# Three real products per complex spectrum product, a head start for the first 256 tokens, and convolution steps handed out by VectorE time

## The chip, the cores and the metric

One core of a Trainium2 chip. The time is device microseconds of one execution, as the median of a few. A profile is one more execution, traced; its span is close to the timed one, not equal. Several chips were used, and the kernel before took 746 to 751 us (medians) on them, so kernels of different sessions are compared by their ratio to the kernel before of the same rounds.

In the profile lines PE is TensorE, PEld its loading of weights, DVE is VectorE, ACT ScalarE and POOL GpSimd; L306 is line 306 of the kernel. In a row of digits each digit is the busy share, in tenths, of one of 40 equal slices of the span. The granted clock (PEclk) is the share of TensorE's full clock that the profile recorded; a cold clock is one of about 0.50. An eviction copies a result out of the memory in which TensorE accumulates.

## The reference

A gated long convolution and then a gated MLP, for 2048 tokens of width 576, hidden width 4608. Cut to what matters:

```python
def _A_ref(q, k, v, shift_k, ssm_k, ssm_D):          # convolution part
    k_shift = sum_t k_pad[:, t:t+S] * shift_k[:, 3-t]
    kv = k_shift * v
    y = irfft(rfft(kv, 2S) * rfft(ssm_k, 2S))[:S] + kv * ssm_D
    return q * y
mod = (silu(c) @ w_mod)                               # six rows: sa, ca, ga, sb, cb, gb
h = layernorm(x) * (1 + ca) + sa
x = x + ga * _A_ref(h, k, v, ...)
h = layernorm(x) * (1 + cb) + sb
x = x + gb * ((silu(h @ w1) * (h @ w3)) @ w2)         # MLP part
```

## The kernel before

The tokens are cut into 8 blocks of 256. The causal convolution is done block by block: TensorE transforms each block of kv to a spectrum X and each block of the long kernel to V, VectorE multiplies X[j] by V[s-j] for each j and sums into the accumulators of block s, and TensorE transforms back. Old spectra are kept in DRAM and read again. The MLP runs in 4 rounds of 512 tokens: 36 hidden blocks (10 matmuls of 512 columns for gate and up together, then silu on ScalarE and the product on VectorE) and a down stage of 288 matmuls of 288 columns. Beside round r's MLP the convolution of round r+1 is threaded in: it is a generator, and the MLP takes a fixed number of its steps after each block.

```python
# one complex product by four real ones: 2304-wide and 1152-wide operations
nc.vector.tensor_mul(p1[:], X[:], V[:])
if not first: nc.vector.tensor_add(a[:], a[:], p1[:])
yield
nc.vector.tensor_mul(p2[:, 0:4:2, :], X[:, 0:4:2, :], V[:, 1:4:2, :])
nc.vector.tensor_mul(p2[:, 1:4:2, :], X[:, 1:4:2, :], V[:, 0:4:2, :])
if not first: nc.vector.tensor_add(b[:], b[:], p2[:])
yield
# ... cut ...
for fc in range(NF // FC):
    for fi in range(FC):
        # ... 10 matmuls, silu, copy, product ...
        interleave(self.rate)            # 2 steps after each hidden block
for h in range(2):
    for f0 in range(0, NF, W2C):         # W2C = 6, two buffers of down weights
        # ... 24 matmuls ...
        interleave(self.rate2)           # 1 step after each down chunk
```

In round 2 there are 72 steps, so two for each of 36 blocks use up all of them beside the hidden stage. A step is anything from an eviction to 2.6 us of VectorE work.

## Time and profile before

| | before |
|---|---|
| median (lowest to highest) | 746.39 us (745.03 to 750.81), 4 runs |
| profiled span | 753.8 us |
| TensorE busy, mean granted clock | 567.0 us, 0.889 |
| VectorE busy | 388.8 us |
| prologue, then the four rounds | 86, 166, 185, 194, 123 us |

A round's length is read from the first gate matmul of one round to that of the next (86.5, 252.0, 437.1 and 630.9 us). The last round has no convolution beside it and so shows what the MLP alone needs.

### The profile page before, as it was taken

Reading aid. Unit: us, or ns where it says so; the run is one execution under the profiler, and the core shown is the slowest. Engines: PE = TensorE matmul, PEld = TensorE weight load, DVE = VectorE, ACT = ScalarE, POOL = GpSimd, SP = SyncE. Lnnn points to the kernel's source line nnn. Section 1 sums busy time; section 2 is a strip of 40 time slices with the busy share of each in tenths; the row PEclk is TensorE's granted clock in tenths of the full one; section 3 lists DMA queues with packets and bytes.
Section 4 is the critical chain, followed back from the end, with each engine's and each line's share of the span. In section 5 each row is a group of like instructions: output and inputs, shape, how many; then the busy total and the mean of one; then the engine's idle time right before and its main releaser. Section 6 shows DMA issues by size and latency. Waiting matters only on the chain.

```text
span 753.8 us, 8712 instructions
## 1 busy us (share of the span) xinstructions
PE 567.0 (75%) x3163; PEld 319.7 (42%) x3201; DVE 388.8 (52%) x708; ACT 254.0 (34%) x503; POOL 24.8 (3%) x44
## 2 busy tenths in 40 slices
PE   0385499549899979815969898984077889999996
PEld 0253244224367534302427654431033565444574
DVE  5668554799301264799940134299998112221111
ACT  3334455333510345314440054522144102445300
POOL 3001000000000000000100000000010000000000
PEclk9867699868999989966889999995579799999999
DMA  8873068713345649841325454694123246544153
GB/s 248 260 245 101 5 193 276 234 31 95 94 134 135 193 148 280 278 135 31 95 63 134 134 173 119 204 266 142 56 60 97 64 126 172 143 128 142 40 140 103
DMA packets 144255, 107.78 MB, mean 143 GB/s; under 512 B 6994, under 2 KB 134868, under 8 KB 144212
## 3 DMA queue, kind: packets, MB, share of 16 engines
q1 hardware_dynamic: 144064, 106.63, 48.2%
q10 hardware_dynamic: 148, 0.59, 0.2%
q8 instruction: 25, 0.41, 0.2%
q14 instruction: 18, 0.15, 0.1%
HBM read 97.17 MB, written 10.03 MB: 142 GB/s over the span
## 4 chain that ended last, share of the span: by engine, by line
PE 41%; DVE 35%; DMA 15%; issue 3%; ACT 3%; POOL 2%; POOLq 0%; SPq 0%; DVEq 0%; ACTq 0%
PE ps L477 24%; PE ps L496 11%; DMA w2t<-in_B_w_dram 10%; DVE zb L313 5%; DVE za L308 4%; PE ps L230 4%; DVE p L306 4%; DVE h L483 2%; DVE p L311 2%; DVE p L310 2%; DMA V<-Vd 2%; POOL l2r L351 2%; DVE xn L366 1%; DVE xn L364 1%; DVE kvt L249 1%
## 5 line engine op out<-in xcount | busy, mean ns | idle before, releaser
L477 PE MATMUL ps<-h2T,wst 128*128 128x512 bf16 x1402 | 340.9, 398 | 12.4 <-ACT u L482 6.2
L477 PEld LDWEIGHTS <-wst 128*128 128x128 bf16 x1440 | 146.5, 102 | 186.6 <-issue 36.8
L480 ACT ACTIVATE sg<-ps 128x512 bf16<-128x512 f32 x144 | 85.9, 596 | 364.6 <-PE ps L477 277.0
L496 PE MATMUL ps<-w2t,h 128*128 128x288 bf16 x1152 | 149.4, 289 | 15.0 <-DMA w2t<-in_B_w_dram 14.8
L483 DVE TENSOR_TENSOR h<-sg,u 128x512 bf16<-128x512 bf16 x144 | 60.8, 423 | 156.4 <-ACT u L482 156.4
L496 PEld LDWEIGHTS <-h 128*128 128x128 bf16 x1152 | 113.5, 99 | 50.3 <-issue 14.5
L504 DVE TENSOR_TENSOR og<-ps,gbrow 128x288 bf16<-128x288 f32 x32 | 13.2, 452 | 143.4 <-PE ps L496 143.4
L482 ACT CAST u<-ps 128x512 bf16<-128x512 f32 x144 | 83.7, 581 | 0.0
L384 PE MATMUL ps<-za,Fb 128*128 128x288 bf16 x64 | 15.7, 333 | 58.4 <-DVE za L374 58.4
L398 PE MATMUL ps<-ident,h2row 128*128 128x128 bf16 x80 | 10.4, 287 | 48.2 <-DVE h2row L367 48.2
L230 PE MATMUL ps<-kv,Fb 128*128 128x288 bf16 x128 | 21.8, 325 | 30.2 <-ACT Fb L139 18.7
L384 PEld LDWEIGHTS <-Fb 128*128 128x128 bf16 x128 | 13.7, 111 | 67.9 <-DVE za L374 61.0
L306 DVE TENSOR_TENSOR p<-X,V 128x2304 bf16<-128x2304 bf16 x28 | 37.9, 1352 | 0.1
L313 DVE TENSOR_TENSOR zb<-zb,p 128x2304 bf16<-128x2304 bf16 x28 | 37.8, 1352 | 0.0
L308 DVE TENSOR_TENSOR za<-za,p 128x2304 bf16<-128x2304 bf16 x28 | 37.8, 1351 | 0.0
L230 PE MATMUL ps<-kT,Fk 128*128 128x288 bf16 x128 | 22.0, 317 | 16.4 <-DVE kT L272 14.8
L341 ACT ACTIVATE junk<-x 128x576 bf16<-128x576 bf16 x32 | 21.9, 685 | 25.1 <-DVE x L390 18.5
L398 PEld LDWEIGHTS <-h2row 128*128 128x128 bf16 x80 | 6.8, 127 | 55.6 <-DVE h2row L367 54.9
L230 PEld LDWEIGHTS <-Fb 128*128 128x128 bf16 x128 | 13.8, 109 | 37.9 <-ACT Fb L139 18.6
L233 ACT CAST W<-ps 128x576 bf16<-128x576 f32 x32 | 19.8, 654 | 20.2 <-PE ps L230 20.1
L351 POOL TENSOR_TENSOR l2r<-l2v,neghalf 128x1 f32<-128x1 f32 x16 | 12.6, 790 | 371.4 <-DVE l2v L350 371.4
L233 ACT CAST X<-ps 128x576 bf16<-128x576 f32 x32 | 19.3, 656 | 13.9 <-PE ps L230 13.9
(81 smaller groups left out, 356.5 us busy)
## 6 DMA issues: line engine op xcount, KB each, us to landing
wst<-in_B_w_dram SPq DMA_DIRECT2D x144, 256.0 KB, 3.4
w2t<-in_B_w_dram SPq DMA_DIRECT2D x48, 432.0 KB, 3.5
X<-Xd SPq DMA_DIRECT2D x15, 576.0 KB, 3.7
V<-Vd SPq DMA_DIRECT2D x12, 576.0 KB, 5.6
kh<-in_A_k_dram SPq DMA_DIRECT2D x7, 720.0 KB, 5.4
wst<-in_B_w_dram SPq DMA_DIRECT2D x144, 32.0 KB, 3.0
Vd<-V SPq DMA_DIRECT2D x7, 576.0 KB, 6.2
h<-in_w_mod_dram SPq DMA_DIRECT2D x6, 576.0 KB, 7.9
```

Source lines behind the costliest of these rows:

```text
L230: nc.tensor.matmul(ps[:, h, 0:H], basis[:, cc, cs, e, :], rhs[:, cc, h * H:(h + 1) * H], start=(cc == 0), stop=(cc == 1))
L233: nc.scalar.copy(dst[:, 2 * e + cs, :].rearrange("p (h d) -> p h d", h=2), ps[:, :, 0:H])
L306: nc.vector.tensor_mul(p1[:], X[:], V[:])
L308: nc.vector.tensor_add(a[:], a[:], p1[:])
L313: nc.vector.tensor_add(b[:], b[:], p2[:])
L351: nc.gpsimd.tensor_tensor(rstd[:], var[:], self.neghalf[:, 0:n], op=ALU.pow)
L384: nc.tensor.matmul(ps[:, h, 0:H], self.Fb[:, e, cs, cc, :], z[:, 2 * e, h * H:(h + 1) * H], start=(e == 0 and cs == 0), stop=(e == 1 and c ...
L477: nc.tensor.matmul(gu[:, i, :], w[:, 5 * i + ct, fi * P:(fi + 1) * P], hT[:, ct, :], start=(ct == 0), stop=(ct == 4))
L480: nc.scalar.activation(sg[:], gu[:, 0, :], ACT.Silu)
L482: nc.scalar.copy(u[:], gu[:, 1, :])
L483: nc.vector.tensor_mul(self.h3[:, f, :], sg[:], u[:])
L496: nc.tensor.matmul(accs[t // 2][:, t % 2, 0:H], self.h3[:, f0 + f, t * P:(t + 1) * P], w[:, f, :], start=(f0 + f == 0), stop=(f0 + f == NF ...
```

## The change

Four things are meant to help: fewer VectorE operations for each complex product (three real products need one sum more for X and two for V, and their spectra have 6 rows instead of 4); steps that carry their VectorE cost, handed out in proportion to the MLP's time; the second block of 256 tokens moved from the prologue to beside the first 20 hidden blocks, which run on the first 256 tokens alone (their weights are read a second time for the other 256); and four smaller buffers for the down weights. The new order of the convolution also puts products that need no new X first. The K transpose's copy moves to ScalarE and the small statistics to GpSimd.

```diff
-W2C = 6
+W2C = 4
+NW2 = 4
+N1 = 20
     def pair(self, X, V, s):
-        nc.vector.tensor_mul(p1[:], X[:], V[:])
-        ... (five operations and two steps, as above)
+        p = self.prod.tile([P, 6, D], BF16, name="p", tag="p")
+        nc.vector.tensor_mul(p[:], X[:], V[:])
+        yield 2.0
+        nc.vector.tensor_add(z[:], z[:], p[:])
+        yield 2.0
     def kv_block(self, s):
+        nc.vector.tensor_add(X[:, 0:6:3, :], X[:, 1:6:3, :], X[:, 2:6:3, :])
     def k_block(self, s):
-        nc.vector.tensor_copy(kT[:], pt[:, :, 0:D])
+        nc.scalar.copy(kT[:], pt[:, :, 0:D])
+        nc.vector.tensor_add(V[:, 2:6:3, :], V[:, 0:6:3, :], VS)
+        nc.vector.tensor_sub(V[:, 1:6:3, :], VS, V[:, 0:6:3, :])
+    def advance(self, cost):
+        self.due += cost
+        while self.due > 0 and self.steps is not None:
+            c = next(self.steps, None)
+            ...
+            self.due -= c
     # after each hidden block, and after each down chunk:
-                interleave(self.rate)
+            self.advance(rate * (t1 - t0) / RB * 2.16)
-                interleave(self.rate2)
+                self.advance(rate * W2C * 4 * 0.126)
     def run(self):
-        for _ in self.conv(0):
+        for _ in self.conv_first():
             pass
+        self.begin(self.conv_second())
+        for fc in range(n1):
+            self.hidden(0, fc, 0, 256, 27.0 / (N1 * 1.08 * 0.9))
+        self.end()
         for r in range(NRB):
-            self.mlp(r, self.steps(r + 1))
+                cost = 4 * (2 * s0 + 1) + 42
+            time = 114.0 * 0.93 - (N1 * 1.08 if r == 0 else 0)
+            rate = cost / time
             ... (cut: hidden blocks, the second half of the first 20, down)
```

## The prediction

> **What bounds the kernel now.** I read the page's busy shares and its slices first, then the engines' busy time by stretch, then the groups of instructions, then the chain of waits in order of time.
>
> ```profile
> PE 567.0 (75%) x3163; PEld 319.7 (42%) x3201; DVE 388.8 (52%) x708; ACT 254.0 (34%) x503; POOL 24.8 (3%) x44
> ...
> PE   0385499549899979815969898984077889999996
> ...
> DVE  5668554799301264799940134299998112221111
> ...
> PEclk9867699868999989966889999995579799999999
> ```
>
> No engine is full over the span, but the two rows of digits are each other's mirror: where VectorE shows 9, TensorE shows 4 to 6 and its clock falls; where TensorE shows 9, VectorE shows 0 to 2. The work alternates, although the code means it to overlap. The stretches (start:end, length, then busy time of PE, PEld, DVE, ACT, POOL, the granted clock, the DMA share, GB/s) put numbers on it. The first five are the prologue and the four rounds of 512 tokens; two convolution-heavy stretches and the hidden stage of the last round follow.
>
> ```profile
> 0.00:87.00 87.00, 34.54 (x202) 23.13 (x204) 61.75 (x129) 33.89 (x67) 11.38 (x27) 0.78 0.61 185
> 87.00:250.00 163.00, 134.59 (x758) 75.47 (x767) 80.84 (x147) 58.62 (x116) 4.22 (x5) 0.91 0.49 142
> 250.00:437.00 187.00, 141.72 (x792) 79.18 (x801) 106.00 (x185) 61.42 (x124) 4.61 (x6) 0.89 0.51 149
> 437.00:631.00 194.00, 142.32 (x778) 78.85 (x786) 118.66 (x193) 61.43 (x124) 4.61 (x6) 0.85 0.45 132
> 631.00:754.00 123.00, 113.81 (x641) 63.08 (x646) 21.57 (x56) 38.65 (x72) 0.00 (x0) 1.00 0.43 122
> 308.00:342.00 34.00, 13.03 (x58) 5.46 (x58) 33.86 (x39) 7.44 (x14) 0.00 (x0) 0.79 0.57 173
> 488.00:543.00 55.00, 26.62 (x105) 10.90 (x105) 54.30 (x62) 12.20 (x23) 0.00 (x0) 0.72 0.57 169
> 631.00:706.00 75.00, 74.63 (x343) 33.97 (x348) 15.69 (x38) 36.50 (x68) 0.00 (x0) 1.00 0.47 133
> ```
>
> The last round, with no convolution beside it, takes 123 us. The three before take 163, 187 and 194. In 488 to 543 VectorE is busy for 54.3 of 55 us and TensorE gets 26.6 us done at a clock of 0.72. VectorE has only 119 us of work in that round of 194: it is the bound for a part of each round and idle in the rest.
>
> ```profile
> L306 DVE TENSOR_TENSOR p<-X,V 128x2304 bf16<-128x2304 bf16 x28 | 37.9, 1352 | 0.1
> L313 DVE TENSOR_TENSOR zb<-zb,p 128x2304 bf16<-128x2304 bf16 x28 | 37.8, 1352 | 0.0
> L308 DVE TENSOR_TENSOR za<-za,p 128x2304 bf16<-128x2304 bf16 x28 | 37.8, 1351 | 0.0
> ...
> L311 DVE TENSOR_TENSOR p<-X,V 128x1152 bf16<-128x1152 bf16 x28 | 21.0, 752 | 0.0
> L310 DVE TENSOR_TENSOR p<-X,V 128x1152 bf16<-128x1152 bf16 x28 | 21.0, 751 | 0.0
> ```
>
> These five are one accumulated spectrum product. The chain of waits steps through them at 1.27 and 0.67 us (each starts 0.08 us before the last ends), and at the down stage it alternates between matmuls and weight loads:
>
> ```profile
> 708.74 2.95 PE ps L496 x24
> 711.71 3.42 DMA w2t<-in_B_w_dram
> 715.17 3.11 PE ps L496 x24
> 718.30 3.54 DMA w2t<-in_B_w_dram
> ```
>
> Two buffers of six row blocks are used up in 6.2 us, while a freed one is refilled only 3.4 us later: a small hole in every second chunk.
>
> **What the Trainium skill says.** "VectorE: DVE Perf Modes", section "The perf-mode tier table", gives tensor_tensor on bf16 in SBUF two elements a cycle and one with a PSUM operand. The trace agrees: (1352 - 752) / 1152 = 0.52 ns an element, and 0.15 us fixed; the 576-wide product that reads PSUM takes 754 ns against 452. So 3456 elements cost about 0.15 + 3456 x 0.52 = 1.95 us, 1.87 as a step of the chain. "TensorE: Matmul & The Clock Gate", section "The HAM clock gate", says that an idle window of about 3.4 us halves the clock; the trace has 0.72 in the VectorE-bound stretch and 1.00 in the last round. "GPSIMD Engine Reference", section "Elementwise — side-by-side cycle accounting", names two software dispatch hops for each GpSimd instruction; the trace has 0.70 to 0.79 us for a power of one or two elements, against 0.15 us for a small VectorE operation. "DMA: Bandwidth & Descriptors", section "Issuing engines are not separate DMA queues", says that all transfers share 16 engines; here 0.47 of them move 133 GB/s of gate and up weights, so about 283 GB/s is all that this kind of load can get.
>
> **The change part by part.**
>
> *Products.* An accumulated product goes from 3 x 1.27 + 2 x 0.67 = 5.15 us to 2 x 1.87 = 3.74. There are 28 of them: 39 us less. The 8 first products go from 2.61 to 1.87: 6 us less. Against this stand a sum for each X (8 x 0.67) and two more operations for each V (16 x 0.67): 16 us more. The K transpose's copy goes to ScalarE (5 us off VectorE) and the small statistics to GpSimd (96 operations of 0.15, 15 us off). VectorE should go from 389 to about 340 us. If VectorE bound everything, this alone would be worth 49 us; the larger effect is the spreading.
>
> *Rounds.* With VectorE off the path, a round is TensorE's: hidden 77.4 us (the last round's, 631.3 to 708.7 in the chain), down 288 x 0.130 = 37.4 (3.12 us for 24 in the chain), and the convolution's own matmuls, two blocks of 48 x 0.1225 + 20 transposes x 0.108 = 16.1 in all (the chain steps through 8 transforms in 0.98 us and 10 transposes in 1.08). Sum 131 us, 115 for the last. VectorE's work beside it is at most about 110 us in round 2 and less before, so it fits if it is spread. The new order of VectorE's instructions does so: one 1.87 us step after each gated product of 0.34 us, 2.2 us per block against TensorE's 2.16. That is nearly balanced, with no clump.
>
> *First 256 tokens alone.* The prologue had both blocks, to 87 us. Now it is block 0 alone, after the modulation matmuls, which wait for 2 MB of weights (transfers issued by 12 us, 7.9 us to land, so about 20 us). I add: transpose and copy of K 5 us, two forward transforms with evictions 8, V and X sums and the product 5, inverse 3, gate, statistics, norm and transpose 10: about 51 us. Then 20 blocks at 256 columns: 200 matmuls of 0.108 = 21.6 us, and 8 us of convolution matmuls. VectorE has 26 operations of 0.67, four of 1.87, 20 small products of 0.21 and some 4 us of others there, about 33 us, and the chain at the end (statistics on ScalarE, five GpSimd operations, norm, transposes) is not covered: I take 40 us. So the second block is ready near 91 us, as late as before, but with 21.6 us of MLP done.
>
> *Second half of those 20 blocks.* Weights are loaded once more, 5.9 MB. A pair of blocks needs 0.59 MB per 2.2 us, 268 GB/s of my 283, and the convolution's own loads come on top: 6 us of waiting.
>
> *Down weights.* Four buffers of four blocks: the 3.4 us of a load lie beside 6.2 us of work. The hole goes: about 3 us a round.
>
> Sum in profile time: 91 for the start; round 0: 34.5 + 22 + 37.4 + 16.1 + 6 + 8 = 124; round 1: 131 + 8 + 2 = 141; round 2: 131 + 8 + 6 = 145; last 117. Total 618. The 8 is a round boundary: the last norm's chain is about 10 us with only 4 us of matmuls left to cover it, and the next x waits for the output to leave (in the old chain 3.15 + 4.20 us). The 2 and 6 are for spectra, which grow by half to 864 KB; in round 2 ten of them come in some 46 us, 193 GB/s on top of the weights' 0.47. The timed runs are 0.991 of the profiled span, so 612; I chose 606, because part of the boundary waits should overlap.
>
> **Rivals.** (1) DMA becomes the bound: the rows above already have 0.57 in product stretches; with spectra half as large again and the step 27% shorter, the demand nearly doubles. Against it: the average over the new span is only some 122 MB / 610 us = 200 GB/s. If it binds in rounds 1 and 2 throughout, 640 to 660. (2) VectorE stays the bound, since sg and u have two buffers and ScalarE waits for VectorE: a delay of one step stops the MLP. The 2.2 against 2.16 speaks for it, the room in the down stages against it: 625. (3) The small operations on GpSimd and the in-order queues lengthen each block's tail: five at 0.5 to 0.8 us, and matmuls placed behind a late transpose stand still: 10 us more at the boundaries. (4) All waits hide: 91 + 110 + 131 + 131 + 115 = 578, timed 573.
>
> **Range and chances.** Predicted 606 us, 8 times in 10 within 580 to 640. Low is nearly rival 4, high is rival 1 half true. Even all rivals together stay far below 746.9, since a round would have to lose over 35 us to them: faster by over 2% 0.98, within 2% 0.01, slower 0.01.
>
> **What would show it.** VectorE's busy time near 340 us, the product and sum rows near 1.95 us, 28 each. Round lengths near 124, 141, 145, 117, with no stretch of VectorE at 9 beside TensorE at 4. First 256-column matmul near 51 us, first 512-column one near 91. Mean clock nearer 0.95 than 0.89. Waits on down weights gone. I am wrong if the rounds stay above 155 us, if the longest waits of TensorE are for spectra or weights, or if the first 512-column matmul comes after 100 us.

## The result, and the profile after

| | before | after |
|---|---|---|
| median (lowest to highest), 4 runs each | 746.39 us (745.03 to 750.81) | 621.99 us (618.59 to 631.15, the last one slow) |
| ratio | 1 | 0.831, 95% interval 0.8255 to 0.8364 |
| profiled span | 753.8 us | 620.6 us |
| VectorE busy | 388.8 us | 341.9 us |
| mean granted clock | 0.889 | 0.956 |

A ratio is the mean time of one kernel's runs over that of the other's of the same rounds, so not quite the ratio of the medians. Executions over 1.5% slower than the fastest of the same kernel are left out of the means. First the page of the changed kernel, busy shares and slices:

```profile
PE 544.3 (88%) x3401; PEld 334.6 (54%) x3401; DVE 341.9 (55%) x534; ACT 268.6 (43%) x551; POOL 45.3 (7%) x104
...
PE   1738858898989698999998788999997979999997
...
DVE  5776576548493457819884338993976131121111
...
PEclk9957989999998989999998979999998989999999
```

The mirror is gone: from the seventh slice on TensorE shows 6 or more in every slice, also where VectorE shows 8 or 9. The same stretches as before, cut at the first matmuls of the changed kernel's stages (prologue, first 256 tokens, rest of round 0, rounds 1 to 3, then 60 us with products in round 2):

```profile
0.00:50.00 50.00, 22.30 (x134) 14.87 (x135) 32.59 (x62) 20.92 (x40) 14.21 (x36) 0.83 0.86 248
50.00:100.50 50.50, 38.47 (x305) 30.30 (x304) 30.67 (x56) 29.86 (x76) 4.90 (x13) 0.89 0.78 237
100.50:216.00 115.50, 104.62 (x751) 72.55 (x749) 70.28 (x114) 49.78 (x113) 6.12 (x15) 0.98 0.80 239
216.00:358.50 142.50, 132.28 (x785) 76.64 (x785) 89.84 (x126) 64.71 (x126) 10.14 (x20) 0.97 0.69 214
358.50:501.50 143.00, 132.13 (x784) 76.70 (x784) 98.33 (x125) 64.70 (x126) 9.89 (x20) 0.97 0.61 184
501.50:620.60 119.10, 114.51 (x648) 63.49 (x647) 20.15 (x52) 38.64 (x72) 0.00 (x0) 0.99 0.42 118
366.00:426.00 60.00, 58.37 (x290) 27.74 (x288) 50.15 (x54) 33.69 (x64) 3.63 (x5) 1.00 0.79 246
```

Rounds 1 and 2 took 185 and 194 us and take 142.5 and 143. In the product stretch VectorE is busy for 50.2 of 60 us, and TensorE for 58.4 at full clock: both at once, where before it was one or the other. The product rows, two where there were five:

```profile
L320 DVE TENSOR_TENSOR p<-X,V 128x3456 bf16<-128x3456 bf16 x28 | 54.7, 1953 | 0.2 <-DMA X<-Xd 0.2
L322 DVE TENSOR_TENSOR z<-z,p 128x3456 bf16<-128x3456 bf16 x28 | 54.7, 1953 | 0.1
```

1953 ns each, and in the whole run 0.2 us of waiting for a spectrum. What is left of TensorE's waits in the rounds stands at their ends. TensorE in order of time, the end of round 0 (start, length, what; in brackets the idle time ahead of it and what ended that):

```profile
205.92 4.08 PE L535 MATMUL ps<-w2t,h 128*128 128x288 bf16 x32
213.25 0.45 PE L410 MATMUL ps<-ident,h2row 128*128 128x128 bf16 x5 [3.25 <-DVE h2row L365]
214.49 0.69 PE L410 MATMUL ps<-ident,h2row 128*128 128x128 bf16 x5 [0.78 <-ACT h2T L412]
215.96 4.43 PE L513 MATMUL ps<-h2T,wst 128*128 128x512 bf16 x10 [0.78 <-ACT h2T L412]
```

The down stage is done, TensorE waits 3.25 us for the last norm, and then its first ten matmuls take 4.43 us instead of 2.3 because the clock has dropped (0.50 granted in 215.9 to 220.2).

### The profile page after: what moved, and what is told of

Same layout as the page of the kernel before. It is cut to its first block, busy times and chain, and to the rows that moved or that the text cites. A ratio compares the mean times of both kernels' runs of the same rounds, so it can differ in the third digit from the quotient of the medians.

```text
span 620.6 us, 9239 instructions
## 1 busy us (share of the span) xinstructions
PE 544.3 (88%) x3401; PEld 334.6 (54%) x3401; DVE 341.9 (55%) x534; ACT 268.6 (43%) x551; POOL 45.3 (7%) x104
## 5 line engine op out<-in xcount | busy, mean ns | idle before, releaser
L513 PE MATMUL ps<-h2T,wst 128*128 128x512 bf16 (+1 forms) x1640 | 325.6, 360 | 6.9 <-DMA wst<-in_B_w_dram 4.5
L513 PEld LDWEIGHTS <-wst 128*128 128x128 bf16 x1640 | 162.0, 99 | 162.3 <-issue 9.9
L516 ACT ACTIVATE sg<-ps 128x512 bf16<-128x512 f32 (+1 forms) x164 | 89.3, 545 | 164.6 <-PE ps L513 158.9
L519 DVE TENSOR_TENSOR h<-sg,u 128x512 bf16<-128x512 bf16 (+1 forms) x164 | 63.4, 390 | 137.0 <-ACT u L518 137.0
L518 ACT CAST u<-ps 128x512 bf16<-128x512 f32 (+1 forms) x164 | 86.7, 528 | 0.0
L339 ACT ACTIVATE junk<-x 128x576 bf16<-128x576 bf16 x32 | 21.9, 684 | 90.9 <-DVE x L397 81.1
L320 DVE TENSOR_TENSOR p<-X,V 128x3456 bf16<-128x3456 bf16 x28 | 54.7, 1953 | 0.2 <-DMA X<-Xd 0.2
L322 DVE TENSOR_TENSOR z<-z,p 128x3456 bf16<-128x3456 bf16 x28 | 54.7, 1953 | 0.1
L410 PE MATMUL ps<-ident,h2row 128*128 128x128 bf16 x80 | 9.6, 271 | 34.5 <-DVE h2row L365 32.1
L240 PE MATMUL ps<-kT,Fk 128*128 128x288 bf16 x128 | 17.5, 286 | 13.5 <-ACT kT L284 10.2
L391 PE MATMUL ps<-z,Fb 128*128 128x288 bf16 x128 | 20.0, 306 | 3.8 <-DVE z L381 3.3
L341 ACT ACTIVATE junk<-x 128x576 bf16<-128x576 bf16 x32 | 21.9, 684 | 1.5
L240 PEld LDWEIGHTS <-Fk 128*128 128x128 bf16 x128 | 12.6, 98 | 18.0 <-issue 14.6
L259 DVE TENSOR_TENSOR kvt<-kh,shk 128x1152 bf16<-128x1152 bf16 x24 | 18.1, 753 | 7.0 <-DMA kh<-in_A_k_dram 7.0
```

Of the source, the lines that this page charges most:

```text
L240: nc.tensor.matmul(ps[:, h, 0:H], basis[:, cc, cs, e, :], rhs[:, cc, h * H:(h + 1) * H], start=(cc == 0), stop=(cc == 1))
L320: nc.vector.tensor_mul(p[:], X[:], V[:])
L322: nc.vector.tensor_add(z[:], z[:], p[:])
L339: nc.scalar.activation(junk[:], src[:, i, :], ACT.Copy, accum_out=ssum[:, i:i + 1])
L341: nc.scalar.activation(junk[:], src[:, i, :], ACT.Square, accum_out=ssq[:, i:i + 1])
L391: nc.tensor.matmul(ps[:, h, 0:H], self.Fb[:, e, cs, cc, :], z[:, 3 * e + cs, h * H:(h + 1) * H], start=(e == 0 and cs == 1), stop=(e == 1 ...
```

## The experiments

The theory from the result, A: VectorE's work no longer sets the length of a round because it is spread over it; TensorE does. The main rival, B: VectorE has less to do, and that is the gain. Others are named where they are tested. Except where said, one part of the changed kernel is undone and the rest kept.

**1. Four products again, steps still by VectorE time.**

```diff
-        nc.vector.tensor_mul(p[:], X[:], V[:]); yield 2.0
-        nc.vector.tensor_add(z[:], z[:], p[:]); yield 2.0
+        # the old five operations, yielding 1.3, 1.3, 1.35 and 1.3; X and V with 4 rows
-                cost = 4 * (2 * s0 + 1) + 42
+                cost = 5.25 * (2 * s0 + 1) + 39
```

> The changed kernel with the old four-product form (three operations of 2304 and two of 1152 for an accumulated product), steps still spread by VectorE time. VectorE's busy time rises from 342 to about 373 us (28 x 1.41 + 8 x 0.74 less 16 for the sums). Theory A (the spreading is what took VectorE off the path; TensorE is the bound of each round and VectorE's work fits beside it in either form): 625 to 635 us against 622, rounds 1 and 2 each at most 5 us longer. Rival B (the shorter product is what counts): the 31 us come back in full, 650 us or more.

Measured: 622.39 us, ratio 0.8306 (0.8268 to 0.8344), the changed kernel's own. VectorE's busy time did rise, to 368.3 us, and none of the 26 us reached the end. B falls for the changed kernel: here the three-product form is worth nothing. A holds, even a little more strongly than expected.

**2. Three products, steps by count.**

```diff
-            self.advance(rate * (t1 - t0) / RB * 2.16)
+            self.count(2 * (t1 - t0) / RB)     # in the rounds
-                self.advance(rate * W2C * 4 * 0.126)
+                self.count(W2C / 6)
```

> The changed kernel with three products, but steps handed out by count as before (two for each block of 512, two thirds for each down chunk of four) in the rounds; the first 256 tokens keep the new rule. All 74 steps of round 2 then fall beside the hidden stage. Theory A: that stage becomes VectorE's, about 94 + 15 = 109 us against 93 for TensorE, so round 2 is some 12 us longer, round 1 some 4, round 0 hardly: 635 to 645. Rival B: at most 627, since the products are short.

Measured: 656.86 us, ratio 0.8757 (0.8714 to 0.88), 35 us more. The direction is A's, the size is larger. Rounds 1 and 2 take 161 and 156 us: round 2 is 13 us longer, as expected, but round 1 is 18 us longer where 4 were expected. The hidden stage of round 2 takes 119 us against 90 in the changed kernel. TensorE waits 46.2 us in all for norms ahead of transposes (32.1 in the changed kernel), 11.9 us for kv and 11.0 us for gate and up weights (4.5).

**3. Both undone, wrongly.** The same two edits together.

> Both undone: four products and steps by count, with the rest of the change kept. Theory A: the two guard against the same bound, so undoing both costs more than the sum of undoing each: 665 to 690, with stretches of VectorE at 9 and TensorE at 4 again. Rival B: the sum of the two single losses.

Measured: 657.27 us, ratio 0.8759. That is neither theory's number, and the reason was in my edit: in run 1's form a product yields four times, so two steps by count are 2.6 us of VectorE work and not 5.2 as in the kernel before. It does not undo what it claims to.

**4. Both undone, with the old two steps a product.**

```diff
         if not first:
-            yield 1.3
             nc.vector.tensor_add(a[:], a[:], p1[:])
-        yield 1.3
+        yield 1.3 if first else 2.6
         ... (the second half likewise)
```

> Mends the third run. There the four-product form gave out four small steps a product (1.3 us each), so two steps for each block were 2.6 us of VectorE work and not 5.2 as in the kernel before. Here a product has its two old steps again, by count, all else as in the third run. Theory A (clumps of VectorE work beside the hidden stage are what costs): round 2 near 185, round 1 near 157, total 680 to 700. Rival D (steps by count cost the same 35 us whatever the product form): 650 to 662.

Measured: 691.34 us, ratio 0.9203 (0.9146 to 0.9259), as A has it; rounds 1 and 2 take 172 and 184 us. The slices show the mirror again, TensorE above, VectorE below:

```profile
PE   2748869984999899384699989774656999999997
...
DVE  5574846898431499977301159999673012111111
```

So with steps by count four products cost 34 us more than three when a product has its two old steps (691 against 657), and nothing more when it has four small ones (run 3, 657 too). VectorE is busy for 369 us in run 3 as in run 4. What costs is how much VectorE work is handed out at once beside one hidden block (5.2 us in run 4, 3.9 in run 2, 2.6 in run 3), not how much there is in all. With steps by time the form is worth nothing.

**5. The kernel before, with steps by VectorE time alone.** Its `yield`s got costs, its product its two old steps of 2.6 us.

```diff
-        def interleave(k):
-            for _ in range(k):
-                if next(steps, None) is None: return
+        rate = (5.25 * (2 * s0 + 1) + 48) / (114.0 * 0.93)
+        def interleave(us):
+            due[0] += rate * us
+            while due[0] > 0:
+                c = next(steps, None)
+                if c is None: return
+                due[0] -= c
```

> The kernel before with one part of the change alone: steps handed out by VectorE time, at a rate that fills 93% of a round; four products, old order of the convolution, no head start. Theory A: rounds 0 to 2 fall from 163, 187, 194 to about 140, 150, 157: 640 to 670. Rival F (the old order of the convolution, with both blocks' transforms ahead of the products, and the buffers hold it back): over 690.

Measured: 652.44 us, ratio 0.8699 (0.8661 to 0.8737). Rounds 0 to 2 take 140, 144 and 158 us. With VectorE still busy for 387.3 us, this one part gives 98 us of what the whole change gives. Forty microseconds of round 2 (start:end, length, busy time of PE, PEld, DVE and so on as above):

```profile
420.00:460.00 40.00, 34.60 (x161) 15.45 (x158) 40.00 (x49) 16.95 (x32) 0.00 (x0) 0.99 0.76 222
```

VectorE is full here, as it was in the kernel before; but now 34.6 us of matmuls fit beside it.

**6. The kernel before, with three products alone.** The old steps; one buffer for the natural-order kernel block instead of two and three for X instead of four, to make room.

```diff
-        nc.vector.tensor_mul(p1[:], X[:], V[:]) ... (five operations)
+        nc.vector.tensor_mul(p[:], X[:], V[:])
+        yield
+        nc.vector.tensor_add(z[:], z[:], p[:])
+        yield
```

> The kernel before with the three-product form alone (and one buffer for the natural-order kernel block instead of two, to make room); steps by count. Theory A: in the old schedule VectorE's clumps are the path, so nearly all of the 30 us of VectorE time that go come back: 715 to 730. Rival B0 (the form is worth nothing in any schedule, as in the changed kernel): 740 or more.

Measured: 750.32 us, ratio 1.0006 (0.9958 to 1.0054). My expectation was wrong. VectorE is busy for 365.0 us, 24 less, but the rounds take 167, 182, 193 and 123 us, against 166, 185, 194 and 123. The chain of waits in order of time shows what took the place, in round 2:

```profile
489.48 4.55 DMA X<-Xd
494.05 1.96 DVE z L304
496.01 1.87 DVE p L310
497.91 6.95 DMA X<-Xd
504.95 1.96 DVE p L310
```

The spectra are half as large again, and with the products in one clump each is needed soon after it is asked for: 4.6 and 7.0 us from issue to landing lie bare on the path. TensorE's waits for gate and up weights also rose, from 2.0 to 12.3 us. The lost X buffer is enough to lay them bare. Each load is issued as the last multiplication by the spectrum before it ends (496.01 + 1.87 = 497.88, issued at 497.91): one buffer turns over, since by the code the spectra of the two new blocks hold the other two. In the kernel before two turn over: there the load issued at 491.42 is for a product that starts at 500.07, and VectorE waits for no old X at all. So this run does not show what three products are worth in the old schedule with all its buffers. A fourth larger one did not fit, so that stays open.

**7. No head start.**

```diff
-N1 = 20
+N1 = 0
```

> N1 = 0: no block runs on the first 256 tokens alone, the second block's convolution is finished first. Theory A: the MLP starts near 86 us, then a full round of 139 us, so round 0 ends near 225 instead of 216: 628 to 634. Rival C (the second load of weights and the half blocks eat the head start): 622 or less.

Measured: 629.91 us, ratio 0.8401 (0.8365 to 0.8437): 8 us, as A has it; a small difference, whose interval only just clears that of the changed kernel (0.8255 to 0.8364). The first hidden block starts at 82.6 us and round 0 ends at 223.3, against 216.0.

**8. Down weights in two buffers of six row blocks.**

```diff
-W2C = 4
-NW2 = 4
+W2C = 6
+NW2 = 2
```

> The changed kernel with the down weights in two buffers of six row blocks, as before. Theory A: the hole of some 0.55 us in every second chunk comes back and, with the extra waits at the ends, 3 us a round: 630 to 636. Rival E (the load hides in either layout once nothing else is late): at most 625.

Measured: 640.72 us, ratio 0.8551 (0.8511 to 0.859): 19 us. A is right in kind and too small. TensorE's waits (who waited for what: us in total, times, longest) say where:

```profile
PE ps L535 <- DMA w2t<-in_B_w_dram: 14.6, 16, 2.7
```

That line is not there at all in the changed kernel. 14.6 us are the direct waits; the last round's down stage is 6 us longer than in the changed kernel (46.2 from its first matmul to the end, against 40.0).

**9. The convolution ends early.** The costs that the steps of a round carry add up to 48 us besides 4 us a product, but the rate is made for 42, so the steps run over to the round's end. Here the rate is made for 54.

```diff
-                cost = 4 * (2 * s0 + 1) + 42
+                cost = 4 * (2 * s0 + 1) + 54
```

> The changed kernel with the cost of a round's convolution put 12 us higher, so that its steps are handed out faster and end before the down stage does. Theory A (the round boundary's 7 us are the last norm's chain, exposed because the steps add up to some 6 us more than the cost they are given, so they run over the end): the waits of 3.25, 0.78 and 0.78 us and about 2.2 us of cold clock go at three boundaries, 600 to 606. Rival G (the waits move: denser VectorE work or the output's and x's transfers hold the next round's start instead): 616 or more.

Measured: 614.89 us, ratio 0.8192 (0.8161 to 0.8223): 9 us of 622 by the ratios, where I expected 16 to 22 (small, but the intervals do not overlap). Rounds 1 and 2 are 136.9 and 138.1 us long, 5 us shorter each. Round 0 gained nothing: its half blocks now wait once for 3.9 us for weights. The norms ahead of the last transposes still cost 1.7 to 1.8 us.

**10. 24 blocks ahead instead of 20.**

```diff
-N1 = 20
+N1 = 24
-            self.hidden(0, fc, 0, 256, 27.0 / (N1 * 1.08 * 0.9))
+            self.hidden(0, fc, 0, 256, 27.0 / (20 * 1.08 * 0.9))
```

> 24 blocks instead of 20 on the first 256 tokens, the steps of the second block at the same pace. Theory A (the 6 us for which TensorE waits for the second block's norm can be filled with four half blocks of 1.1 us): 616 to 620. Rival H (the weights of four more blocks are loaded twice and transfers are near their limit there, as the waits of 1.7 and 1.1 us show): 622 or more.

Measured: 624.49 us, ratio 0.8314 (0.8284 to 0.8343): no gain, rival H's number. But its reason is not shown: TensorE still waits 5.09 us for the second block's norm (6.07 before), so the added blocks did not land where the wait is, and its waits for gate and up weights rose only from 4.5 to 5.9 us.

**11. Gaps where TensorE waited.** One MLP block between a K transpose and its transforms, more down matmuls between a norm and its transposes.

```diff
             self.load_k(s + 1)
-        yield 0.2
+        yield 2.6
             self.norm2(s, 0, 2)
-            yield 2.4
+            yield 6.0
-                cost = 4 * (2 * s0 + 1) + 42
+                cost = 4 * (2 * s0 + 1) + 54
```

> One MLP block set between a K transpose and its transforms (TensorE waits 1.2 to 1.6 us there for ScalarE's copy, six times), and more down matmuls between a norm and its transposes (2.5 to 3.3 us, three times); the convolution's end stays where it is. Theory A: those 16 us of waits go, less what still ends late: 606 to 612. Rival I (the instruction order is made by a scheduler that undoes such gaps, or the wait moves to the next transform): 618 or more.

Measured: 603.31 us, ratio 0.8033 (0.7983 to 0.8082), 19 us less than the changed kernel. The end of round 1 reads:

```profile
344.79 4.94 PE L535 MATMUL ps<-w2t,h 128*128 128x288 bf16 x39
349.57 0.44 PE L410 MATMUL ps<-ident,h2row 128*128 128x128 bf16 x5
350.79 0.44 PE L410 MATMUL ps<-ident,h2row 128*128 128x128 bf16 x5 [0.78 <-ACT h2T L412]
352.01 2.32 PE L513 MATMUL ps<-h2T,wst 128*128 128x512 bf16 x10 [0.78 <-ACT h2T L412]
```

The 3.25 us are gone, and with them the cold clock: the first ten matmuls take 2.32 us. The waits for the K copy, 10.2 us in the changed kernel, are gone too; those for norms ahead of transposes fall from 32.1 to 21.4 us. The edit makes both gaps at once, so this split is read from the waits and not tested. The norms inside the down stage still cost 2.0, 2.6 and 2.3 us. Rounds 1 and 2 take 134.3 and 133.6 us; the prediction's TensorE sum was 131.

**12. All three.**

```diff
-N1 = 20
+N1 = 24
     ... (the rate of 10, the yields of 11)
-                cost = 4 * (2 * s0 + 1) + 42
+                cost = 4 * (2 * s0 + 1) + 66
```

> The three together: 24 blocks ahead, gaps, and the convolution ending early. If the waits are independent: 622 - 19 - 4 - 13 = 586, range 580 to 596. If they are the same waits told three times: 600 or more.

Measured: 599.40 us, ratio 0.7999 (0.7959 to 0.8039). It beats both given kernels, but its interval overlaps that of run 11, so the step beyond 11 is unclear. Measured apart, the three gave 9, 0 and 19 us or a little over; together they give 23, so the waits are in part the same ones. All twelve kernels gave correct results.

Put together, medians in us (the two rows of the new kernel have the new order of the convolution, the head start and the new down buffers):

| | steps by count | steps by VectorE time |
|---|---|---|
| kernel before, four products | 751 | 652 |
| kernel before, three products | 750, with an X buffer fewer | not run |
| changed kernel, four products | 691 in two steps a product, 657 in four | 622 |
| changed kernel, three products | 657 | 622 |

The parts measured singly are 98 us (spreading, in the kernel before), 8 (head start) and 19 (down buffers, both in the changed kernel), 125 of 124 to 128; as they come from different kernels the sum is a rough account. The new order of the convolution, the K copy on ScalarE and the small statistics on GpSimd were not tested apart.

## Why the prediction was right

606 us was predicted, 622 came, inside the range of 580 to 640. The sum by stages, in profile time:

| stage | predicted, us | trace, us |
|---|---|---|
| first 256-column matmul | 51 | 49.9 |
| first 256 tokens alone | 40 | 46.3 (to the next convolution's K transposes at 96.2) |
| rest of round 0 | 124 | 119.7 |
| round 1 | 141 | 142.5 |
| round 2 | 145 | 143.1 |
| last round | 117 | 119.1 |
| sum | 618 | 620.6 |

*What bounds.* Right: TensorE bounds the rounds. "The larger effect is the spreading" holds, and more than I said: run 5 has 98 us from the spreading alone, run 1 has nothing from the product form once the work is spread. The mirror of the two rows of digits was told too neatly: in the nine slices where VectorE shows 9, TensorE shows 4, 9, 1, 5, 9, 8, 4, 0 and 7. The stretches carry the argument, not the digits.

*Products.* The sizes were right (1.95 us predicted, 1953 ns; VectorE 340 predicted, 341.9). The sentence that 49 us would come back "if VectorE bound everything" was not borne out by a run: the 34 us between runs 4 and 2 go with the size of the steps (run 3), and run 6, which should have shown it in the kernel before, also lost an X buffer.

*First 256 tokens.* Too short by 6 us. The end of the chain was sized at about 7 us over the other work; the trace has 6.07 us of waiting for the norm, 1.2 us for the K copy, 2.7 us for weights, and cold matmuls after that (16 of 256 columns in 4.28 us where a warm ten take 1.25). With the next block's K transforms put ahead, the first 512-column matmul came at 100.5 us, just past the 100 that I had named as a sign of error; the error is this stage's.

*Second half of those blocks.* I had 6 us of waiting for weights; the trace has single waits of 1.1, 0.3, 0.3 and 0.2 us.

*Round boundaries.* The 8 us were right in size and mostly right in cause: 3.25 + 0.78 + 0.78 us of waits and 2.1 us of cold clock. Run 11 removes the first and the cold clock and shows that these are the norm's chain. The x transfer, which I had added, is not among TensorE's waits.

*Spectra in rounds 1 and 2.* The 2 and 6 us did not appear: 0.2 us in all. In their place stand the K copy (10.2 us over the run) and the norms inside the down stage (2.5 to 3.3 us a round, each with a cold clock after it), which I had not listed.

*Down weights.* 3 us a round was too small: run 8 has 19 us, and its rounds are 2.2, 4.1, 3.4 and 6.8 us longer in the traces.

*The step from 618 to 606.* This is what cost the 16 us. I scaled by 0.991 because the kernel before ran that much faster timed than traced, and took 6 us more off for overlap. But the execution that was traced took 755.55 us by the timer, 1.8 us more than its span, as the changed kernel's traced one did (622.44 for 620.6). It was one slower than the other four (745 to 751); the 0.991 was the spread between executions, not a scale between trace and timer. And little overlapped: a boundary cost 6.9 us of the 8. The unscaled sum was the better number. That it fell within 3 us of the traced span is partly luck: the first 256 tokens came 6 us longer than predicted and the rest of round 0 4 us shorter.

*Rivals.* The first (DMA) did not come: 0.2 us of waiting for spectra in the changed kernel, and run 6 cannot tell it from the lost buffer. The second (VectorE still the bound) is refuted by run 1, which adds 26 us of VectorE work at no cost. The third (block tails, 10 us at the boundaries) is borne out by run 11, where the waits for norms fall by 10.7 us, 8.8 of them at the boundaries; what the GpSimd operations have in it was not tested apart. The K copy, the other half of what that run gained, was in no rival. The fourth, 573 with all waits hidden, was not reached: the best run has 599.

## What to carry to other kernels

When two engines take turns although the code threads one's work between the other's, look first at how the steps are handed out: by count they clump, by time they fit, and that alone gave 98 of the 124 to 128 us here. Once they fit, making that work cheaper gave nothing: the changed kernel has 26 us less VectorE work than run 1 and takes as long. An experiment that gives up a buffer to make room tests the buffer too, as run 6 did. Once the work is spread, the remaining waits sit where a short chain over several engines ends in an instruction placed too early on the busiest one; a few more of its own instructions ahead of that place cost nothing and gave 19 us.

## What the Trainium skill lacked or had wrong

- "TensorE: Matmul & The Clock Gate", section "Why this matters for your kernels", warns of idle gaps above about 3 us. Here shorter ones were enough when five transposes followed: after a wait of 2.54 us for a norm the next six down matmuls took 1.65 us where warm ones take 0.13 us each, and after another of 2.54 us (ended at 329.4) the granted clock was 0.51 from 330.2 to 333.6. There is no sharp limit: in run 12 a wait of 2.50 us (ended at 442.9) left the clock full. At the boundary, after 3.25 + 0.78 + 0.78 us ten matmuls took 4.43 us, after 0.78 + 0.78 us alone 2.32.
- "GPSIMD Engine Reference", section "Elementwise — side-by-side cycle accounting", has no cost for a few elements. The small statistics of two elements took on average 0.19 us (multiply and add), 0.21 to 0.74 us (subtract) and 0.72 to 0.78 us (power) in the changed kernel's trace.
- No page that I read says how a second stream of work should be handed out when it is threaded into an engine's queue; by count instead of by time cost 35 us in run 2 and 98 us in the kernel before (run 5).
